# One list of rows per expert against two: first and second visits of a token in a fused attention and mixture-of-experts kernel

## The chip, the cores and the metric

The kernel runs on one core of one Trainium2 chip. The metric is the device time of one execution in microseconds (us). Each engine of the core has its own instruction stream: TensorE (PE) multiplies matrices, VectorE (DVE) and ScalarE (ACT) work elementwise, GpSimd (POOL) here issues the indirect transfers and the weight loads, and SyncE (SP) issues plain transfers. They wait for each other through semaphores.

## The reference, cut to what matters

Linear attention over q, k, v gives x with 4608 rows (tokens) of 512. A noisy router then chooses two of eight experts for each row, and the output is the weighted sum of the two experts' results.

```python
def _attn_ref(q, k, v):                  # each (8, 8, 576, 64)
    phi = lambda x: np.where(x > 0, x, np.exp(x) - 1.0) + 1.0
    q_p, k_p = phi(q), phi(k)
    kv = np.einsum('bhsd,bhse->bhde', k_p, v)
    z = np.sum(k_p, axis=2)
    num = np.einsum('bhsd,bhde->bhse', q_p, kv)
    den = np.einsum('bhsd,bhd->bhs', q_p, z)[..., None] + 1e-06
    return num / den
# x: (4608, 512); w1: (8, 512, 1024); w2: (8, 1024, 512)
logits = x @ w_gate
noisy_logits = logits + np.log1p(np.exp(x @ w_noise)) * noise
top2 = np.argpartition(-noisy_logits, 2, axis=1)[:, :2]
# top2_w: softmax over the two chosen logits
out = np.zeros((4608, 512))
for e in range(8):
    for k in range(2):
        mask = top2[:, k] == e
        h = np.maximum(x[mask] @ w1[e], 0.0)
        out[mask] += top2_w[mask, k, None] * (h @ w2[e])
```

The experts are computed in order of their number, so of a token's two experts the lower one is its first visit and the higher one its second.

## The kernel before

Attention and routing are done in groups of 1152 tokens. After each group, `dispatch` scatters its rows, with the gates and the token's number behind the 512 values, to `x_sorted`, a scratch array in device memory with one list for each expert:

```python
    def dispatch(self, u, a=0, z=9):

        tc = self.tc
        g, c0, c1 = UNITS[u]
        for ci in range(c0 + a, min(c1, c0 + z)):
            for sl in range(2):
                self.nc.gpsimd.nop()
                r = self.nc.gpsimd.indirect_dma_start(
                    out=self.x_sorted,
                    out_offset=bass.IndirectOffsetOnAxis(ap=self.r["posi", u][:, ci - c0, sl : sl + 1], axis=0),
                    in_=self.xr[g % 2][:, ci, :].bitcast(INT32), in_offset=None,
                )
# ...
```

Room for 1216 rows of each list is computed; a branch at the end handles longer lists. Experts 0 to 7 follow. A row tile of 128 passes four steps: load and transpose, `mm1` with w1 and relu, `mm2` with w2, and the output. Outside expert 0, each tile first clears a buffer `L`, then gathers what its tokens' first visit has written to `out` (a first visit's index lies out of bounds, so its row stays zero), adds, and scatters the sum to `out`:

```python
    def zero_l(self, b):
        for t in range(b["nt"]):
            b["L"][t] = self.lp.tile([P, HD], FP32, name="L")
            self.nc.vector.memset(b["L"][t][:], 0.0)

    def gather(self, b):

        nc, tc = self.nc, self.tc
        gi = self.m[b["key"]][2]
        for t in range(b["nt"]):
            m, tt = self.rows(b, t), b["t0"] + t
            nc.gpsimd.nop()
            r = nc.gpsimd.indirect_dma_start(
                out=b["L"][t][0:m].bitcast(INT32), out_offset=None, in_=self.out.bitcast(INT32),
                in_offset=bass.IndirectOffsetOnAxis(ap=gi[0:m, tt : tt + 1], axis=0),
                bounds_check=N_TOK - 1, oob_is_err=False,
            )
            g = f"own{b['e']}"
            tc.declare_no_dep(r.ins, group=g, reason="the rows of one expert are of distinct tokens")
            tc.add_to_no_dep_group(g, r.ins)

    def mm1(self, b, *fcs):
        nc, n = self.nc, b["n"]
        w1 = self.w[b["e"]][0]
        if "hT" not in b:
            b["hT"] = self.hp.tile([P, 8, 512], BF16, name="hT")
        for fc in fcs:
            ps = self.rot(self.ps_h, "h").tile([P, 512], FP32, name="b")
            for dc in range(4):
                nc.tensor.matmul(out=ps[:, 0:n], lhsT=w1[:, dc, fc * P : fc * P + P], rhs=b["xt"][:, dc, 0:n],
                                 start=(dc == 0), stop=(dc == 3))
            nc.scalar.activation(out=b["hT"][:, fc, 0:n], in_=ps[:, 0:n], func=ACT.Relu)

    def mm2(self, b, t):
        nc = self.nc
        w2 = self.w[b["e"]][1]
        m = self.rows(b, t)
        gate, tt = self.m[b["key"]][0], b["t0"] + t
        ps = self.rot(self.ps_y, "y").tile([P, HD], FP32, name="b")
        for fc in range(8):
            nc.tensor.matmul(out=ps[0:m], lhsT=b["hT"][:, fc, t * P : t * P + m], rhs=w2[:, fc, :],
                             start=(fc == 0), stop=(fc == 7))
        y = b["y", t] = self.rot(self.yp, "yy").tile([P, HD], FP32, name="y")
        if t in b["L"]:
            nc.vector.scalar_tensor_tensor(out=y[0:m], in0=ps[0:m], scalar=gate[0:m, tt : tt + 1],
                                           in1=b["L"][t][0:m], op0=ALU.mult, op1=ALU.add)
        else:
            nc.vector.tensor_scalar(out=y[0:m], in0=ps[0:m], scalar1=gate[0:m, tt : tt + 1], scalar2=None, op0=ALU.mult)

    def scatter(self, b, t):
        nc, tc = self.nc, self.tc
        m, tt = self.rows(b, t), b["t0"] + t
        si = self.m[b["key"]][1]
        nc.gpsimd.nop()
        r = nc.gpsimd.indirect_dma_start(
            out=self.out, out_offset=bass.IndirectOffsetOnAxis(ap=si[0:m, tt : tt + 1], axis=0),
            in_=b["y", t][0:m], in_offset=None, bounds_check=N_TOK - 1, oob_is_err=False,
        # ... (all scatters of an expert must have landed before the next expert gathers)
```

`interval` interleaves `mm1` of the current block (up to 512 rows) with `mm2` and the output of the block before. Two early blocks of expert 0, `r1` with 512 rows and `r2` with 256, are read before the dispatch is complete: after groups 1 and 2 the list's counter is raised to 512 and 768, so that later rows go behind that bound. Their rows are transposed by the DMA engines (`xt_load`); other blocks are transposed by TensorE (`xn_t`). At the end of the attention:

```python
    pa.ps_misc = pa.ps_misc[:1]
    col = c["rowpos"]
    pa.num(3, 0, 1)
    pa.num(3, 1, 0)
    pa.num(3, 1, 1)
    pa.num(3, 2, 0)
    pa.rt_a(3)
    pa.num(3, 2, 1)
    pa.rt_b(3)
    pb.mm1(r1, 0)
    pa.rt_c(3)
    pa.dispatch(3)
    pa.rt_a(4)
    pb.mm1(r1, 1)
    pa.rt_b(4)
    pb.mm1(r1, 2)
    pa.rt_c(4)
    pa.dispatch(4)
    pb.mm1(r1, 3, 4, 5, 6, 7)
    pb.meta("r1", c["cnt"][0][:], col[:, 0:4], code_of(0))
    pb.interval(r2, r1)
    pb.meta("r2", c["cnt"][1][:], col[:, 4:6], code_of(0))
    return r2
```

Then the blocks of the experts:

```python
        blocks = [pb.block(0, 768, CAP - 768, 0, 6, True)]
        for e in range(1, E):
            blocks += [pb.block(e, r, n, e, r // P) for r, n in ((0, 512), (512, 512), (1024, CAP - 1024))]
        pb.meta_load(0, 0, T_CAP)
        pb.xt_load(blocks[0])
        for i, b in enumerate(blocks):
            nxt = blocks[i + 1] if i + 1 < len(blocks) else None
            for nb in blocks[i + 1 : i + 3] if i == 0 else blocks[i + 2 : i + 3]:
                pb.xn_load(nb)
                if nb["row"] == nb["e"] * REGION:
                    pb.meta_load(nb["e"], nb["row"], T_CAP)
            if i == 0 or b["e"] != blocks[i - 1]["e"]:
                e = b["e"]
                pb.meta(e, c["carry"][:, e : e + 1], c["rowpos"][:], code_of(e))
            todo = []
            if e + 2 < E and (i == 0 or b["e"] != blocks[i - 1]["e"]):
                pb.w_tiles(e + 2, 1 if e + 2 < 6 else 0)
                todo = [(e + 2, part) for part in range(4)]
            pb.interval(b, prev, todo, nxt)
            prev = b
        pb.interval(None, prev)
    pb.overflow()
```

Of the kernel before, what the change touches and what calls it, by code (L numbers as in the profile page):

```python
# [7 lines left out]
FP32 = mybir.dt.float32  # L8
# [7 lines left out]
P = 128  # L16
# [6 lines left out]
CAP = 1216  # L23
T_CAP = 10

UNITS = [(0, 0, 9), (1, 0, 9), (2, 0, 9), (3, 0, 6), (3, 6, 9)]

ROUNDS = [(1, 512), (2, 768)]
REGION = N_TOK
ROW_W = 576  # L30
BIG = 1.0e6
# [8 lines left out]


def code_of(e):
    return float(E - e) / E


def build_constants(tc, consts, w_gate, w_noise, noise):
# [22 lines left out]
    )  # L69
    ut = c["ut"] = tile_("ut", [P, P], BF16)  # L70
# [25 lines left out]
    carry = c["carry"] = tile_("carry", [P, E])  # L96
    nc.vector.memset(carry[:], 0.0)
    c["cnt"] = [tile_(f"cnt{i}", [P, 1]) for i in range(len(ROUNDS))]
# [7 lines left out]
class PhaseA:  # L106


    def __init__(self, ctx, tc, q, k, v, x_sorted, psum):
        self.tc, self.nc = tc, tc.nc  # L110
        self.src, self.x_sorted = {"q": q, "k": k, "v": v}, x_sorted
        self.ps_num, self.ps_misc = psum
        self.turn = 0
        pool = lambda name, bufs: ctx.enter_context(tc.tile_pool(name=name, bufs=bufs, side="right"))
        self.kq = pool("A_kq", 3)
        self.pers = pool("A_pers", 1)
        self.v = [self.pers.tile([P, 12, S], BF16, name=f"v{i}") for i in range(2)]
        self.ep = pool("A_e", 2)
        self.kvp, self.kvt = pool("A_kvp", 2), pool("A_kvt", 1)
        self.pq = pool("A_pq", 5)  # L120
        self.rt = pool("A_rt", 1)
        self.x, self.e, self.kvps, self.kvbd, self.pqt, self.r, self.ps = {}, {}, {}, {}, {}, {}, {}
# [161 lines left out]
    def rt_b(self, u):  # L284
# [3 lines left out]
        t4 = lambda name, dt=FP32: self.rt.tile([P, 2, 9, E], dt, name=name)[:, :, 0:n]  # L288
# [3 lines left out]
        noisy, eq, oh, mx, code = t3("noisy"), t3("eq"), t4("oh"), t2("mx"), t2("code")  # L292
# [4 lines left out]
        for sl in range(2):  # L297
# [4 lines left out]
            nc.vector.tensor_tensor(out=oh[:, sl], in0=c8b, in1=bc(code, sl), op=ALU.is_equal)  # L302
            if sl == 0:
                nc.vector.scalar_tensor_tensor(out=noisy, in0=oh[:, 0], scalar=-1e30, in1=noisy,
                                               op0=ALU.mult, op1=ALU.add)
        A = t3("A", BF16)
        nc.vector.tensor_tensor(out=A, in0=oh[:, 0], in1=oh[:, 1], op=ALU.add)
        rps = self.misc()
        rk = rps[:, 0 : 8 * n].rearrange("p (a b) -> p a b", a=n)
        tt = rps[:, 256 : 256 + 8 * n].rearrange("p (a b) -> p a b", a=n)  # L310
        nc.tensor.matmul(out=rk, lhsT=c["ut"][:], rhs=A, start=True, stop=False, skip_group_check=True)
        nc.tensor.matmul(out=tt, lhsT=c["ones"][:], rhs=A, start=False, stop=False, skip_group_check=True)
# [3 lines left out]
        dl = t1("dlt")  # L316
        nc.vector.tensor_tensor(out=dl, in0=mx[:, 1], in1=mx[:, 0], op=ALU.subtract)
        meta = _ap(self.xr[g % 2], [[ROW_W, n], [1, 16]], off=c0 * ROW_W + HD).bitcast(FP32)
# [4 lines left out]
        nc.scalar.copy(out=fld(3), in_=code[:, 0])  # L323
        r.update(oh=oh, code=code, rps=rps, rk=rk, dl=dl)

    def rt_c(self, u):
# [3 lines left out]
        t2 = lambda name: self.rt.tile([P, 2, 9], FP32, name=name)[:, :, 0:n]  # L330
        pos, pr = self.rt.tile([P, 9, E], FP32, name="pos")[:, 0:n], self.rt.tile([P, 2, 9, E], FP32, name="pr")[:, :, 0:n]
        rank, posf, key = t2("rank"), t2("posf"), t2("key")
        tot, gs = self.rt.tile([P, E], FP32, name="tot"), self.rt.tile([P, 9], FP32, name="gs")[:, 0:n]
        nc.vector.tensor_scalar_add(out=gs, in0=r["dl"], scalar1=1.0 + 1e-9)
        nc.vector.reciprocal(out=gs, in_=gs)
        fld = r["fld"]
        nc.vector.tensor_tensor(out=pos, in0=r["rk"], in1=_ap(c["carry"], [[0, n], [1, E]]), op=ALU.add)
        nc.vector.tensor_tensor(out=fld(1), in0=r["dl"], in1=gs, op=ALU.mult)
        nc.vector.tensor_tensor(out=pr, in0=r["oh"], in1=_ap(pos, [[0, 2], [E, n], [1, E]]), op=ALU.mult)
        nc.vector.tensor_tensor(out=fld(2), in0=gs, in1=fld(1), op=ALU.subtract)  # L340
        nc.vector.tensor_reduce(out=rank, in_=pr, op=ALU.add, axis=AX.X)

        nc.vector.scalar_tensor_tensor(out=key, in0=rank, scalar=float(CAP), in1=r["code"],
                                       op0=ALU.is_ge, op1=ALU.subtract)
        nc.vector.scalar_tensor_tensor(out=posf, in0=r["code"], scalar=float(-REGION * E), in1=rank,
                                       op0=ALU.mult, op1=ALU.add)
        nc.vector.tensor_tensor(out=fld(4), in0=key[:, 0], in1=key[:, 1], op=ALU.is_lt)
        posi = r["posi", u] = self.rt.tile([P, 9, 2], INT32, name="posi", bufs=2)
        nc.vector.tensor_scalar_add(out=_ap(posi, [[1, 2], [2, n]]), in0=posf, scalar1=float(E * REGION))
        nc.vector.tensor_reduce(out=tot[:], in_=_ap(r["rps"], [[1, E], [E, n]], off=256), op=ALU.add, axis=AX.X)  # L350
        nc.vector.tensor_tensor(out=c["carry"][:], in0=c["carry"][:], in1=tot[:], op=ALU.add)
        for i, (after, q) in enumerate(ROUNDS):
            if after == u:
                c0_ = c["carry"][:, 0:1]
                nc.vector.tensor_copy(out=c["cnt"][i][:], in_=c0_)
                nc.vector.tensor_scalar_max(out=c0_, in0=c0_, scalar1=float(q))

    def dispatch(self, u, a=0, z=9):
# [3 lines left out]
        for ci in range(c0 + a, min(c1, c0 + z)):  # L362
            for sl in range(2):
# [7 lines left out]
                for i, (after, q) in enumerate(ROUNDS):  # L371
                    if after < u:
                        tc.declare_no_dep(r.ins, group=f"read{i}", reason="that round reads rows below its bound")
                tc.add_to_no_dep_group("disp", r.ins)


class PhaseB:


    def __init__(self, ctx, tc, w1, w2, x_sorted, out):  # L380
        self.tc, self.nc = tc, tc.nc
        self.w1, self.w2, self.x_sorted, self.out = w1, w2, x_sorted, out
# [5 lines left out]
        self.ps_h = self.ps_y = None  # L388
        self.count = {}
        self.w, self.m = {}, {}  # L390
# [22 lines left out]
    def meta_load(self, key, row, nt, group=None):  # L413
        m = self.mp.tile([P, nt, 8], INT32, name=f"meta{nt}")
        rows = self.x_sorted[row : row + nt * P, HD // 2 : HD // 2 + 8]
        r = self.nc.sync.dma_start(out=m[:], in_=rows.rearrange("(t p) c -> p t c", p=P))
        if group:
            self.tc.add_to_no_dep_group(group, r.ins)
        self.m[key] = (m, nt)

    def meta(self, key, n_e, rowpos, code):

        nc, mp = self.nc, self.mp
        mi, nt = self.m[key]
        m = mi[:].bitcast(FP32)
        t2 = lambda name, dt=FP32: mp.tile([P, nt], dt, name=f"{name}{nt}")
        gate, inv, isf, si, gi = t2("gate"), t2("inv"), t2("isf"), t2("si", INT32), t2("gi", INT32)
        nc.vector.tensor_scalar(out=inv[:], in0=rowpos, scalar1=n_e, scalar2=BIG, op0=ALU.is_ge, op1=ALU.mult)
        nc.vector.scalar_tensor_tensor(out=gate[:], in0=m[:, :, 3], scalar=code, in1=m[:, :, 2],
                                       op0=ALU.is_equal, op1=ALU.mult)  # L430
        nc.vector.scalar_tensor_tensor(out=isf[:], in0=m[:, :, 3], scalar=code, in1=m[:, :, 4],
                                       op0=ALU.is_equal, op1=ALU.is_equal)
        nc.vector.tensor_tensor(out=si[:], in0=mi[:, :, 0], in1=inv[:], op=ALU.max)
        nc.vector.tensor_tensor(out=gate[:], in0=gate[:], in1=m[:, :, 1], op=ALU.add)
        nc.vector.scalar_tensor_tensor(out=gi[:], in0=isf[:], scalar=BIG, in1=si[:], op0=ALU.mult, op1=ALU.max)
        self.m[key] = (gate, si, gi)

    def block(self, e, row, n, key, t0, first=False):
        return {"e": e, "row": e * REGION + row, "n": n, "key": key, "t0": t0, "first": first,
                "nt": -(-n // P), "L": {}}  # L440

    def xt_load(self, b, group=None):
        n = b["n"]
        b["xt"] = self.xp.tile([P, 4, 512], BF16, name="xt")
        src = self.x_sorted[b["row"] : b["row"] + n, 0 : HD // 2].bitcast(BF16)
        r = self.nc.sync.dma_start(out=b["xt"][:, :, 0:n], in_=src, transpose=True)
        if group:
            self.tc.add_to_no_dep_group(group, r.ins)

    def xn_load(self, b):  # L450

        n, nc = b["n"], self.nc
        b["xn"] = self.np.tile([P, 4, HD], BF16, name="xn")
        k = n // P
        src = lambda a, z: self.x_sorted[b["row"] + a : b["row"] + z, 0 : HD // 2].bitcast(BF16)
        nc.sync.dma_start(out=b["xn"][:, 0:k], in_=src(0, k * P).rearrange("(t p) d -> p t d", p=P))
# [361 lines left out]
```

## Time and profile before

| | us |
|---|---|
| median of 3 runs | 472.89 (471.3 to 472.99) |
| span of the profiled execution | 493.9 |
| TensorE busy | 367.1 (74%) |
| GpSimd busy | 269.7 (55%) |
| VectorE busy | 209.7 (42%) |
| ScalarE busy | 187.0 (38%) |
| scatters to x_sorted, 72 | 76.1 |
| scatters to out, 80 | 79.0 |
| gathers from out, 70 | 71.2 |
| clearing of L, 70 | 34.0 |

Times of single stretches are those of the profiled execution, which is longer than the timed runs. A row of the profile names the line of the kernel, the engine, the operation and the tiles (output <- input), how often it occurs, busy time and mean duration, and what ended the idle time before it. The chain of waits goes back from the last instruction of the execution, at each step to what released it. "issue" there is time in which an engine waited for nothing that the profile shows, and "another core or an unknown queue" a release that it can't name. PEclk is the clock granted to TensorE, where 1.00 is full speed. In the table by stage, the columns after the stretch and its length are busy us (and instructions) of PE, of its weight loads, of DVE, ACT and POOL, then the clock, the DMA share and GB/s.

### The profile page before, as it was taken

What the parts mean: (1) busy time and instruction counts of PE and PEld (TensorE: products, weight loads), DVE (VectorE), ACT (ScalarE), POOL (GpSimd) and SP (SyncE); (2) the same over time, 40 slices, a digit from 0 to 9 for tenths busy, and PEclk for the clock granted to TensorE, in tenths of its full rate; (3) what the DMA queues carried; (4) which work ended last, traced back from release to release, by engine and by line L of the source; (5) the groups of instructions that cost most, each with busy time, mean ns of one, the idle gap of its engine ahead of it and who ended that gap; (6) DMA issues with size and microseconds to landing.
All of it is one profiled execution on the core that took longest, in us unless ns stands there. A gap on an engine that the chain in (4) does not pass through costs nothing.

```text
span 493.9 us, 6809 instructions
## 1 busy us (share of the span) xinstructions
PE 367.1 (74%) x2513; PEld 208.2 (42%) x2513; DVE 209.7 (42%) x526; ACT 187.0 (38%) x304; POOL 269.7 (55%) x289
## 2 busy tenths in 40 slices
PE   0395354554332159999979999999997999999980
PEld 0284253443311014544634554554543554454540
DVE  1928999695672102431351351351260342242330
ACT  1537564513110022544325345345335336235310
POOL 6121258877667712437568547557467555546550
PEclk9997777666557559999998999999998999999995
DMA  9999993993974345395958846956956955434440
GB/s 138 207 238 210 208 224 96 216 211 109 167 214 141 119 84 162 114 225 116 212 175 165 205 149 144 240 152 145 249 183 152 255 182 156 144 126 116 156 142 2
DMA packets 69035, 82.12 MB, mean 166 GB/s; under 512 B 24981, under 2 KB 54997, under 8 KB 68992
## 3 DMA queue, kind: packets, MB, share of 16 engines
q0 software_dynamic: 40448, 69.90, 60.2%
q1 hardware_dynamic: 26880, 11.51, 10.6%
q10 hardware_dynamic: 1664, 0.18, 0.5%
q8 instruction: 21, 0.34, 0.3%
q14 instruction: 22, 0.18, 0.1%
HBM read 88.55 MB, written 31.74 MB: 244 GB/s over the span
## 4 chain that ended last, share of the span: by engine, by line
PE 62%; DVE 13%; DMA 10%; issue 4%; another core or an unknown queue 4%; ACT 4%; POOL 1%; POOLq 0%; ACTq 0%
PE b L512 29%; PE b L523 28%; DMA kq<-in_q_dram 7%; PE t L472 3%; DVE xr L254 3%; DMA x_sorted<-xr,posi 2%; DVE e L161 2%; ACT e L151 2%; PE num L243 1%; DVE kq L158 1%; DVE lwt L261 1%; DVE kvbd L192 1%; ACT hT L514 1%; PE misc L227 1%
## 5 line engine op out<-in xcount | busy, mean ns | idle before, releaser
L512 PE MATMUL b<-xt,w 128*128 128x512 bf16 (+3 forms) x768 | 158.1, 350 | 25.6 <-issue 19.3
L514 ACT ACTIVATE hT<-b 128x512 bf16<-128x512 f32 (+3 forms) x192 | 96.0, 510 | 163.2 <-PE b L512 110.4
L523 PE MATMUL b<-w,hT 128*128 128x512 bf16 (+1 forms) x640 | 150.9, 379 | 0.0
L537 POOL DMA_INDIRECT out_dram<-y,si x80 | 79.0, 988 | 99.0 <-DVE y L527 37.5
L527 DVE SCALAR_TENSOR_TENSOR y<-b,gate,L 128x512 f32<-128x512 f32 x70 | 51.5, 743 | 172.9 <-PE b L523 106.5
L512 PEld LDWEIGHTS <-w 128*128 128x128 bf16 x768 | 72.5, 101 | 94.8 <-issue 42.5
L365 POOL DMA_INDIRECT x_sorted<-xr,posi x72 | 76.1, 1057 | 34.2 <-issue 19.2
L495 POOL DMA_INDIRECT L<-out_dram,gi x70 | 71.2, 1017 | 38.1 <-issue 21.7
L523 PEld LDWEIGHTS <-hT 128*128 128x128 bf16 (+1 forms) x640 | 62.3, 99 | 69.0 <-issue 3.4
L151 ACT ACTIVATE e<-kq 128x2304 bf16<-128x2304 bf16 x16 | 33.1, 2122 | 21.2 <-DMA kq<-in_k_dram 9.2
L476 ACT COPY xt<-t 128x1024 bf16<-128x1024 bf16 x28 | 28.3, 1011 | 24.9 <-PE t L472 14.9
L486 DVE MEMSET L<- 128x512 f32 x70 | 34.0, 485 | 4.2 <-ACT xt L476 0.3
L180 PE MATMUL misc<-v,e 64*128 64x192 bf16 x144 | 19.9, 314 | 20.9 <-DVE e L161 20.9
L180 PEld LDWEIGHTS <-e 64*128 64x128 bf16 x288 | 21.6, 124 | 30.3 <-DVE e L161 28.7
L243 PE MATMUL num<-kvbd,pqt 128*64 128x162 bf16 x288 | 19.6, 311 | 19.5 <-DVE lwt L261 16.2
L472 PE MATMUL t<-ident,xn 128*128 128x128 bf16 x280 | 21.7, 219 | 6.0 <-ACT xt L476 6.0
L243 PEld LDWEIGHTS <-pqt 128*64 128x64 bf16 x288 | 16.2, 153 | 22.1 <-DVE lwt L261 13.1
L180 PE MATMUL b<-v,e 64*128 64x192 bf16 x144 | 20.0, 314 | 7.0 <-DVE e L161 4.9
L472 PEld LDWEIGHTS <-xn 128*128 128x128 bf16 x280 | 18.5, 99 | 15.3 <-issue 6.6
L254 DVE TENSOR_TENSOR xr<-num,rden 128x384 bf16<-128x384 f32 x48 | 23.4, 550 | 0.4
L161 DVE TENSOR_TENSOR e<-e,kq 128x2304 bf16<-128x2304 bf16 x16 | 21.3, 1354 | 0.3
L530 DVE TENSOR_SCALAR y<-b,gate 128x512 f32<-128x512 f32 (+1 forms) x10 | 7.5, 750 | 27.2 <-PE b L523 27.2
(108 smaller groups left out, 214.5 us busy)
## 6 DMA issues: line engine op xcount, KB each, us to landing
w<-in_moe_w_dram POOLq DMA_DIRECT2D x32, 512.0 KB
xn<-x_sorted SPq DMA_DIRECT2D x14, 512.0 KB
kq<-in_k_dram POOLq DMA_DIRECT2D x8, 576.0 KB
kq<-in_q_dram POOLq DMA_DIRECT2D x8, 576.0 KB
v<-in_v_dram POOLq DMA_DIRECT2D x8, 576.0 KB
out_dram<-y,si POOLq DMA_INDIRECT x80
x_sorted<-zrow SPq DMA_DIRECT2D x8, 144.0 KB
x_sorted<-xr,posi POOLq DMA_INDIRECT x72
```

Of the source, the lines that this page charges most:

```text
L151: self.nc.scalar.activation(out=e, in_=x, func=ACT.Exp)
L180: nc.tensor.matmul(out=self.kvps[g, h, j][:, KVM * i : KVM * i + KVM], lhsT=e[half, hp, ci, :], rhs=v[half, hp::4, 64 * ci : 64 * ci + 64] ...
L243: nc.tensor.matmul(out=ps[half, hp, KVW * i : KVW * i + KVW], lhsT=self.pqt[g, 3 * t + i][:, hp, half], rhs=self.kvbd[g][:, j, hp, :], sta ...
L254: nc.vector.tensor_tensor(out=_ap(xr, [[ROW_W, 3], [256, 2], [1, 64]], off=3 * t * ROW_W + 64 * hp), in0=_ap(ps, [[KVW, 3], [64, 2], [1, 6 ...
L365: r = self.nc.gpsimd.indirect_dma_start(out=self.x_sorted, out_offset=bass.IndirectOffsetOnAxis(ap=self.r["posi", u][:, ci - c0, sl : sl + ...
L472: nc.tensor.transpose(ps[:, i, dc, 0:m], b["xn"][0:m, t, dc * P : dc * P + P], self.c["ident"][0:m, 0:m])
L495: r = nc.gpsimd.indirect_dma_start(out=b["L"][t][0:m].bitcast(INT32), out_offset=None, in_=self.out.bitcast(INT32), in_offset=bass.Indirec ...
L512: nc.tensor.matmul(out=ps[:, 0:n], lhsT=w1[:, dc, fc * P : fc * P + P], rhs=b["xt"][:, dc, 0:n], start=(dc == 0), stop=(dc == 3))
L514: nc.scalar.activation(out=b["hT"][:, fc, 0:n], in_=ps[:, 0:n], func=ACT.Relu)
L523: nc.tensor.matmul(out=ps[0:m], lhsT=b["hT"][:, fc, t * P : t * P + m], rhs=w2[:, fc, :], start=(fc == 0), stop=(fc == 7))
L527: nc.vector.scalar_tensor_tensor(out=y[0:m], in0=ps[0:m], scalar=gate[0:m, tt : tt + 1], in1=b["L"][t][0:m], op0=ALU.mult, op1=ALU.add)
L537: r = nc.gpsimd.indirect_dma_start(out=self.out, out_offset=bass.IndirectOffsetOnAxis(ap=si[0:m, tt : tt + 1], axis=0), in_=b["y", t][0:m] ...
```

## The change

Each expert gets two lists: F, the rows for which it is the first visit, and S, those for which it is the second. A first visit no longer touches `out`: its result is stored plainly to a scratch array `part`, in the order of the list. A second visit gathers the token's row of `part`, adds, and writes `out` once. Nothing has to be cleared, and no gather waits for scatters to `out`. A row carries where its first visit lies. Expert e computes `N_F[e]` full tiles of F, `N_S[e]` of S, and 192 "mid" rows (M), gathered from the ends of both lists; expert 0 has only F and expert 7 only S. Three experts, not one, have early rows in two rounds: 512, 384 and 256 rows of experts 0, 1 and 2, then up to 768, 640 and 512. A memset of a spare tile on GpSimd now follows each indirect transfer. The weights of experts 0 and 1 are loaded between dispatches of groups 1 and 2. No row is transposed by DMA engines any more.

The core of the diff (cut; the router's ranking now counts 16 lists in the same way):

```diff
-ROUNDS = [(1, 512), (2, 768)]
+N_F = [8, 7, 6, 5, 3, 2, 1, 0]
+N_S = [8 - n for n in N_F]
+ROUNDS = [(1, (512, 384, 256)), (2, (768, 640, 512))]
+EARLY = 3
 # constants
+    c["gap"], c["gap2"] = tile_("gap", [P, 192]), tile_("gap2", [P, 352])
 # dispatch, after each scatter
+    def apart(self):
+        self.nc.gpsimd.memset(self.c["gap"][:], 0.0)
 # attention, in the loop over groups
-        pa.dispatch(g, 0, 6 if g == 0 else 9)
-        if g > 0:
-            rd = (r1, r2)[g - 1]
-            pb.meta_load(rd["key"], (0, 512)[g - 1], rd["nt"], f"read{g - 1}")
-            pb.xt_load(rd, f"read{g - 1}")
+        if g == 0:
+            pa.dispatch(0, 0, 6)
+        else:
+            pb.w_tiles(g - 1)
+            for i in range(4):
+                pa.dispatch(g, 2 * i, 2 * i + 2)
+                pb.w_load(g - 1, i)
+            pa.dispatch(g, 8, 9)
 # gather, for S and M tiles alone
-            r = nc.gpsimd.indirect_dma_start(
-                out=b["L"][t][0:m].bitcast(INT32), out_offset=None, in_=self.out.bitcast(INT32), ...
+            if kind == "F":
+                continue
+            L = b["L"][t] = self.lp.tile([P, HD], FP32, name="L")
+            nc.gpsimd.nop()
+            r = nc.gpsimd.indirect_dma_start(
+                out=L[0:m].bitcast(INT32), out_offset=None, in_=self.part.bitcast(INT32), ...
+            nc.gpsimd.memset(self.c["gap2"][:], 0.0)
 # the output of a tile
-    def scatter(self, b, t):
+    def put(self, b, t):
+        if kind != "S":
+            row = e * REGION + (N_F[e] if kind == "M" else 0) * P + i * P
+            r = nc.sync.dma_start(out=self.part[row : row + m], in_=y[0:m])
+        if kind != "F":
+            nc.gpsimd.nop()
+            r = nc.gpsimd.indirect_dma_start(out=self.out, ...)     # as before
+            nc.gpsimd.memset(self.c["gap2"][:], 0.0)
 # interval
-        if cur and new and not cur["first"]:
-            self.gather(cur)
+        if nxt:
+            self.gather(nxt)
 # the end of the routing, with the early blocks
+    a0, a1 = first, pb.block(1, ("F", 0, 3))
+    b0, b1 = pb.block(0, ("F", 4, 2)), pb.block(1, ("F", 3, 2))
+    a2, c0 = pb.block(2, ("F", 0, 4)), pb.block(0, ("F", 6, 4))
+    ...
+    pb.mm1(a0, 0)
+    pa.rt_b(3)
+    pb.mm1(a0, 1, 2)
+    pa.rt_c(3)
+    pa.dispatch(3)
+    pa.rt_a(4)
+    pb.mm1(a0, 3, 4, 5)
+    pa.rt_b(4)
+    pb.mm1(a0, 6, 7)
+    pa.rt_c(4)
+    pa.dispatch(4)
+    pb.mids()
+    ...
+    pb.interval(a1, a0, (), b0)
+    pb.w_load(2, 0, 1, 2, 3)
+    pb.interval(b0, a1, (), b1)
+    pb.prepare(0)
+    pb.xn_load(c0)
+    pb.interval(b1, b0, (), a2)
+    pb.w_tiles(3, 1)
+    pb.w_load(3, 0, 1, 2, 3)
+    pb.interval(a2, b1, (), c0)
 # the later blocks: kind, first tile, tiles
+PLAN = {
+    1: [[("F", 5, 2)], [("M", 0, 1), ("S", 0, 1), ("M", 1, 1)]],
+    2: [[("F", 4, 2)], [("M", 0, 1), ("S", 0, 2), ("M", 1, 1)]],
+    3: [[("F", 0, 4)], [("F", 4, 1), ("M", 0, 1), ("S", 0, 1), ("M", 1, 1)], [("S", 1, 2)]],
+    ...
+    7: [[("S", 0, 4)], [("S", 4, 4)], [("S", 8, 2)]],
+}
```

## What was predicted

> **What bounds the kernel now.** I read the 40 slices first, then busy time by stage, the chain of work in order of time, the waits, and the GpSimd timeline. The slices show two kernels in one.
>
> ```profile
> PE   0395354554332159999979999999997999999980
> POOL 6121258877667712437568547557467555546550
> PEclk9997777666557559999998999999998999999995
> ```
>
> From slice 15 (185 us) on, TensorE is nearly always busy at full clock: the experts are bound by it. Before, during attention and routing, it is mostly idle at a reduced clock, while GpSimd is busiest in slices 7 to 13, where it scatters rows to the sorted lists. The stage table (length, then busy us of each engine) sets the sizes:
>
> ```profile
> 137.00:155.00 18.00, 7.31 (x27) 2.64 (x27) 11.54 (x58) 2.53 (x10) 12.12 (x13) 0.61 0.58 183
> 155.00:181.00 26.00, 4.03 (x9) 1.22 (x9) 2.87 (x22) 2.14 (x4) 15.80 (x17) 0.56 0.34 107
> 181.00:480.00 299.00, 289.39 (x1664) 148.24 (x1662) 97.67 (x204) 122.88 (x229) 167.62 (x173) 0.98 0.67 169
> 480.00:494.00 14.00, 0.00 (x0) 0.00 (x0) 0.17 (x1) 0.00 (x0) 0.92 (x1) 0.58 0.06 22
> ```
>
> From 155 to 181 us TensorE works 4 us of 26. The chain says how:
>
> ```profile
> 151.04 3.77 PE b L512 x8
> 154.81 9.11 issue
> 163.92 0.60 ACT hT L514
> 164.52 9.88 another core or an unknown queue
> 174.42 0.60 ACT hT L514
> 175.02 5.02 another core or an unknown queue
> 180.06 0.61 ACT hT L514
> 180.70 4.42 PE b L512 x12
> ```
>
> The first block of expert 0 has begun, but ScalarE and VectorE hardly advance, with no wait the profile can name. The stretch lies over GpSimd's unbroken row of dispatch scatters and ends with them:
>
> ```profile
> 173.46 0.96 POOL L365 DMA_INDIRECT x_sorted<-xr,posi  x1 [0.30 <-issue]
> 174.72 0.96 POOL L365 DMA_INDIRECT x_sorted<-xr,posi  x1 [0.30 <-issue]
> 188.55 0.99 POOL L537 DMA_INDIRECT out_dram<-y,si  x1 [12.87 <-DVE y L530]
> ```
>
> A scatter takes 0.96 and 0.30 passes before the next, so 1.27 us each. Even without stalls, only 768 early rows of expert 0 could be computed before the last scatter lands. Later, the read-modify-write of the output costs something too. GpSimd's longest waits in the expert stage:
>
> ```profile
> POOL L L495 <- DMA out_dram<-y,si: 14.6, 5, 6.2
> POOL out_dram L537 <- issue: 10.1, 31, 0.9
> POOL out_dram L537 <- DVE gate L429: 6.9, 5, 2.3
> ```
>
> The first line is five gathers of a new expert held up by the scatters of the old one; VectorE additionally waits 14.8 us for gathers at L527. TensorE itself lists only about 12 us of waits after 181 us.
>
> [...] granted clock 0.50 from 175 to 185 us, and the twelve matmuls from 180.70 take 4.42 us, 0.37 each, against 0.216 later. [...] From 120 to 200 us each instruction queue shows one packet, so I don't take the stall for a shortage of instructions.
>
> **The change part by part.** (1) *TensorE work.* Eight experts keep 1216 rows and ten tiles each. Up-projection: 8 x 1216 x 32 columns, or 608 matmuls of 512 columns at 0.216 us (eight take 1.73 us in the chain): 131 us. Down-projection: 80 tiles x 1.73: 138 us. Transposes: three DMA transposes become forty more on TensorE, 320 in all, eight in 0.44 us: 18 us, of which 2.2 are new. Sum 287 us, nearly unchanged; smaller blocks (256, 320, 384 columns) cost nothing extra, since eight matmuls of 192 columns already take only 0.67 us.
>
> (2) *Early rows.* Instead of 512 + 256 rows of expert 0, 512 + 256 of expert 0, 384 + 256 of expert 1 and 512 of expert 2 may be computed before the dispatch has ended: 1920 rows. A row costs 64 columns, so 1920 x 64 x 0.422 ns = 52 us, plus 3 for transposes, against 21 before. Work for 34 us more is available exactly where TensorE stood idle.
>
> (3) *Dispatch.* A GpSimd memset of 192 elements now follows each of 72 scatters. A memset of 128 elements took 0.20 us and one of 1 element 0.10, so I estimate 0.25 us for 192, and 72 x 0.25 = 18 us. Weight loads of experts 0 and 1 move between scatters, adding nothing overall. The last scatter thus moves from 176 to about 188 us: attention leaves slack at first, and roughly 12 of the 18 us show. If the unbroken row of scatters is what holds up the others, the spaces also release ScalarE and VectorE.
>
> (4) *What early work waits for.* TensorE starts at about 144 us, as now. [...] The second early round needs the third group's scatters, about 160 us, and its load, about 166; TensorE reaches it at 159: 7 us lost. Expert 2's weights are issued only after the last scatter. Four loads of 1 MB each took some 15 us to land after 93 us, so the first two land near 198, while TensorE arrives near 190: 8 us lost.
>
> (5) *Expert stage.* The 70 memsets of L (34 us of VectorE) go, off the path. Indirect transfers fall from 150 to 104: 46 gathers, 46 scatters and 12 for mixed tiles; 46 plain stores go to SyncE. GpSimd needs 104 x (1.0 + 0.3 + about 0.38) = 175 us, against about 195 before, in a stage of some 270: not a bound. A gather now waits only for plain stores of earlier experts and is issued a block ahead. TensorE lost 299 - 289 = 10 us idle plus about 6 at low clock; I leave 6 in all.
>
> (6) *End.* Last scatter and final test stay: 14 us.
>
> Sum for a profiled execution: 144 + 287 + 3 + 7 + 8 + 6 + 14 = 469, against 493.9: 25 us less. The timed runs before are 21 us below the profiled span. Some of the unnamed stall may exist only under the profiler, so I do not carry all 25 over, but 19: 472.9 - 19 = 454 us.
>
> **The rivals.** *The stall belongs to the profiler.* The 21 us between profile and timed runs are suspiciously like the stall of 26. Then the timed kernel before already did all its 21 us of early work and waited only for the dispatch; the gain is the wait left over, some 15 us, minus the later dispatch: 465 to 472. Against it: the spaces in the new code suggest that closely packed transfers hurt something. *The dispatch becomes the bound.* If memset and switching cost 0.6 us and not 0.25, the last scatter lands near 205 us, the weights of expert 2 near 222, and TensorE stands idle again: 470 to 480. For it: GpSimd is the busiest engine from 65 to 176. *Stores and gathers collide.* SyncE takes stores and row loads in order, so a store waiting for VectorE delays the next load; TensorE would show short waits in every expert. Rows are loaded two blocks ahead, which speaks against it; three microseconds an expert would give 478. *Better than thought.* The attention stage also has stalls of 3.5 and 3.4 us near 117 to 125, in the chain, within a row of scatters; spaces may remove these, and the experts may lose nothing: 441.
>
> **Range and chances.** The central sum gives 454. The good rival and half of its gain again set the lower end, 439; the profiler rival sets the upper end, 470. Faster by over 2% means below 463.4: I give 0.70. Within 2%: 0.19. Slower needs dispatch or SyncE to become a bound: 0.11.
>
> **What would show it.** Right: TensorE busy most of 150 to 210 us; the last dispatch near 188; scatter spacing near 1.5 us; no unnamed waits of ScalarE for 10 us; expert stage 290 us or less from there on; GpSimd's waits for out_dram gone. Wrong: first matmul of expert 0 well after 144 (attention delayed by spaced dispatches), spacing of 1.8 or more, TensorE waiting for w over 15 us at expert 2, or repeated waits for xn, xm or L in later experts. If the stall is gone but the timed gain is under 10 us, the profiler rival was right.

## The result, and the profile after

The changed kernel takes 455.35 us (median of 4 runs, 454.04 to 456.05). Beside it the kernel before takes 472.22 us (471.3 to 472.99). The ratio is 0.964, with a 95% interval from 0.9609 to 0.9671. Ratios, here and below, leave out disturbed executions, so that those of `b_pet` and of the runs on chip 10 are not quite the quotients of the medians. The profiled span is 453.6 us. The number predicted was 454, and the range held it; the reasons need more sorting than that suggests.

The same three rows of the 40 slices as before (now 11.3 us each):

```profile
PE   0195475564626879799999999999999899999991
POOL 7130229888888888710065637469658867776883
PEclk9998868668558899899999999999999999999997
```

TensorE is busy from slice 12 (137 us) on and no longer from slice 15 (185 us). The hole with digits 3, 3, 2 and 1 is gone, although GpSimd's row of scatters (slices 6 to 15) is denser than it was. The table by stage:

```profile
137.00:145.00 8.00, 6.68 (x30) 3.00 (x31) 3.69 (x23) 4.32 (x11) 7.05 (x12) 0.78 0.86 216
145.00:181.00 36.00, 29.83 (x182) 17.24 (x185) 11.88 (x55) 13.24 (x28) 31.74 (x51) 0.95 0.72 213
181.00:211.00 30.00, 26.65 (x153) 13.60 (x155) 2.60 (x6) 14.15 (x25) 10.99 (x16) 0.94 1.12 223
211.00:440.00 229.00, 226.15 (x1343) 121.99 (x1365) 54.87 (x114) 100.54 (x190) 148.18 (x208) 1.00 0.72 191
440.00:454.00 14.00, 4.38 (x20) 1.77 (x18) 2.25 (x3) 0.00 (x0) 5.48 (x9) 0.78 0.22 80
```

From 137 to 181 us TensorE works 36.5 us of 44; before, it worked 11.3 in the same stretch. All that it waits for between 137 and 215 us, one row for each cause (total, times, longest):

```profile
PE t L586 <- DMA xn<-x_sorted: 2.8, 2, 2.3
PE misc L331 <- DVE A L326: 2.3, 1, 2.3
PE b L624 <- DMA w<-in_moe_w_dram: 2.1, 1, 2.1
PE b L624 <- ACT xt L590: 1.3, 2, 1.1
PE t L586 <- ACT xt L590: 1.3, 2, 1.1
PE b L624 <- ACT xt L592: 0.7, 1, 0.7
PE b L624 <- issue: 0.4, 2, 0.2
```

Between 60 and 215 us no unnamed wait ("issue", or "remote": another core or an unknown queue) above 0.2 us is left on TensorE, ScalarE and VectorE. Last, GpSimd's timeline at the end of the dispatch; the bracket is the idle time before the instruction:

```profile
177.74 0.97 POOL L387 DMA_INDIRECT x_sorted<-xr,posi  x1 [0.16 <-issue]
178.71 0.28 POOL L378 MEMSET gap<- 128x192 f32 x1
179.15 0.97 POOL L387 DMA_INDIRECT x_sorted<-xr,posi  x1 [0.17 <-issue]
```

One scatter starts 1.41 us after the other (1.27 before). The memset takes 0.27, but the idle time ahead of a scatter falls from 0.30 to 0.17, so the memset costs 0.14 us net. The last scatter starts at 179.15; in the profile of before it was 174.72.

### The profile page after: what moved, and what is told of

It reads as the page before. It is cut to its first block, busy times and chain, and to the rows that moved or that the text cites. A ratio compares the mean times of both kernels' runs of the same rounds, so it can differ in the third digit from the quotient of the medians.

```text
span 453.6 us, 7034 instructions
## 1 busy us (share of the span) xinstructions
PE 361.4 (80%) x2554; PEld 215.8 (48%) x2585; DVE 179.3 (40%) x481; ACT 193.0 (43%) x313; POOL 285.4 (63%) x425
## 4 chain that ended last, share of the span: by engine, by line
PE 38%; POOL 29%; DMA 18%; issue 5%; DVE 5%; ACT 2%; POOLq 0%; ACTq 0%; DVEq 0%
PE b L624 18%; PE b L635 18%; POOL x_sorted L387 14%; DMA kq<-in_q_dram 8%; POOL gap L378 4%; POOL L L607 4%; DMA w<-in_moe_w_dram 3%; DMA xn<-x_sorted 3%; POOL out_dram L655 3%; PE t L586 3%; DMA xm<-x_sorted,m_idx 2%; ACT e L169 2%; POOL gap L614 2%; POOL gap L661 1%; DMA x_sorted<-xr,posi 1%
## 5 line engine op out<-in xcount | busy, mean ns | idle before, releaser
L624 PE MATMUL b<-xt,w 128*128 128x512 bf16 (+5 forms) x787 | 148.7, 333 | 5.3 <-DMA w<-in_moe_w_dram 2.1
L626 ACT ACTIVATE hT<-b 128x512 bf16<-128x512 f32 (+5 forms) x200 | 97.0, 496 | 113.5 <-PE b L624 111.6
L590 ACT COPY xt<-t 128x1024 bf16<-128x1024 bf16 x32 | 32.4, 1012 | 56.3 <-PE t L586 56.0
L655 POOL DMA_INDIRECT out_dram<-y,si x34 | 33.9, 997 | 14.4 <-DVE y L639 8.9
L607 POOL DMA_INDIRECT L<-part,mgi x12 | 12.0, 1004 | 49.0 <-DMA xn<-x_sorted 35.6
L607 POOL DMA_INDIRECT L<-part,gi x34 | 34.7, 1021 | 9.2 <-issue 9.2
L586 PE MATMUL t<-ident,xn 128*128 128x128 bf16 (+1 forms) x256 | 20.9, 221 | 4.2 <-DMA xn<-x_sorted 2.8
L586 PEld LDWEIGHTS <-xn 128*128 128x128 bf16 (+1 forms) x256 | 17.3, 99 | 13.4 <-DMA xn<-x_sorted 3.8
L655 POOL DMA_INDIRECT out_dram<-y,msi x12 | 11.7, 979 | 18.9 <-DVE y L639 13.7
L639 DVE SCALAR_TENSOR_TENSOR y<-b,mgate,L 128x512 f32<-128x512 f32 (+1 forms) x12 | 9.0, 746 | 32.8 <-PE b L635 32.8
```

Of the source, the lines that this page charges most:

```text
L586: nc.tensor.transpose(ps[:, i, dc, 0:m], self.xn(b, t, dc), self.c["ident"][0:m, 0:m])
L590: nc.scalar.copy(out=b["xt"][:, :, t * P : t * P + 2 * P].rearrange("p c (i r) -> p i c r", i=2), in_=ps)
L607: r = nc.gpsimd.indirect_dma_start(out=L[0:m].bitcast(INT32), out_offset=None, in_=self.part.bitcast(INT32), in_offset=bass.IndirectOffset ...
L655: r = nc.gpsimd.indirect_dma_start(out=self.out, out_offset=bass.IndirectOffsetOnAxis(ap=self.m[e, kind, i]["si"][0:m], axis=0), in_=y[0:m ...
```

## The experiments

**Theory A:** the time before is set by the last dispatch scatter, behind which TensorE has nothing to do; early rows of three experts fill that wait, and the memsets cost what they delay. **Rival B:** the memsets (called spaces from here) end the unnamed stall, and that is the gain. **Rival C:** the gain lies in the output path, in gathers that no longer wait for scatters. **Rival D:** the gain is the transposes taken from the DMA engines.

The runs fell on four chips, and these differ. On chip 7 the kernel before takes 472.5 us, as in the result above; on chips 13, 10 and 15 it takes 492 to 494. So each ratio below is against the kernel before on the same chip.

### Chip 7: spaces added, spaces removed, early rows removed

`b_gap`: the kernel before, with one line more.

```diff
                     in_=self.xr[g % 2][:, ci, :].bitcast(INT32), in_offset=None,
                 )
+                self.nc.gpsimd.memset(self.c["gap"][:], 0.0)     # 128 x 192, a spare tile
```

> The kernel before, with the memset of 192 elements after each of the 72 dispatch scatters and nothing else. Theory A (the unnamed stall from 155 to 181 us exists only under the profiler; the timed kernel before waits for the last scatter): the profiled span falls by 15 to 25 us from 493.9, because the stall goes, while the timed median does not fall; it rises by 3 to 10 us, since 72 x 0.135 us (1.405 against 1.27 us a scatter) put the last scatter about 10 us later. Theory B (the spaces release ScalarE and VectorE in timed runs too): the timed median falls by 8 us or more. Theory C (two lists make the gain): the timed median stays within 3 us.

Measured: 481.5 us against 472.54, ratio 1.0196 (1.0167 to 1.0226). The last scatter starts at 183.99 us. The spacing is 1.405 us instead of 1.27, so 72 spaces make 72 x 0.135 = 9.7 us of later dispatch, and the time grows by 9.0. That fits a kernel that its dispatch bounds almost one to one (9.7 is worked out; the kernel before was not profiled on chip 7). Rival B is wrong for this chip; spaces alone cost. Two stages of this run, and what TensorE and then GpSimd waited for:

```profile
145.00:193.00 48.00, 24.08 (x98) 10.76 (x99) 9.72 (x55) 8.67 (x21) 39.52 (x62) 0.71 0.47 147
193.00:465.00 272.00, 270.22 (x1560) 140.15 (x1591) 92.46 (x187) 118.08 (x218) 162.38 (x169) 0.99 0.70 179
```

```profile
PE b L514 <- DMA xt<-x_sorted: 29.4, 3, 13.3
```

```profile
POOL L L497 <- DMA out_dram<-y,si: 31.8, 8, 8.4
```

This decides on rival C too. In the experts GpSimd waits 31.8 us for scatters to `out` before it may gather, and TensorE still works 270.2 of 272 us: these waits lie beside the matmuls. In this stretch the old output path cost TensorE at most 1.8 us. TensorE's long waits from 137 us on, 29.4 us together, are for transposed rows: before the first early matmul (12.6), in the second round (3.5), and behind the last early row:

```profile
193.03 3.17 PE L514 MATMUL b<-xt,w 128*128 128x448 bf16 x8 [13.33 <-DMA xt<-x_sorted]
```

This last wait is mostly one for the dispatch: the rows are loaded from 187.01 us on, after the last scatter.

`a_nogap1` and `a_nogap`: the changed kernel without the 72 spaces of the dispatch, and without these and the memsets behind the later gathers and scatters.

```diff
     def apart(self):
-        self.nc.gpsimd.memset(self.c["gap"][:], 0.0)
+        pass
 # a_nogap alone, three places:
-            nc.gpsimd.memset(self.c["gap2"][:], 0.0)
```

> The changed kernel without the memset after the dispatch scatters; the memsets after the later gathers and scatters stay. Theory A: timed 450 to 457 us, as with it or slightly faster, since the last scatter comes some 10 us earlier and TensorE hardly waits for it; the profiled span grows by 10 us or more above 453.6, because the stall returns. Theory B: the timed median rises by 8 us or more, to 463 or above.

> The changed kernel without any of the memsets, neither after dispatch scatters nor after the later gathers and scatters. Theory A: 448 to 457 us timed, no worse than the changed kernel. Theory B: 463 us or more, and more than without the first kind alone if closely packed gathers and scatters hold up the experts as well.

Measured: 447.86 us, ratio 0.9471 (0.9413 to 0.9528), and 445.82, ratio 0.9436 (0.9412 to 0.9461). The profile of `a_nogap` has no unnamed wait of ScalarE or VectorE between 60 and 215 us, though its scatters stand 1.27 us apart. On this chip the spaces cost 7 to 10 us of the 455. The last scatter starts at 169.73 in `a_nogap`, 9.4 us earlier, but that is not how they cost: the changed kernel has early rows until 208 us, and TensorE doesn't wait for the last scatter. It starts its early work 4.2 us later with spaces (133.5 and 137.76), and then idles 10.8 us up to 211 instead of 7.2 up to 199. The memsets in the expert stage are not told apart from nothing: the intervals of the two runs overlap.

`a_early1`: the changed kernel, spaces kept, with early rows of expert 0 alone.

```diff
-ROUNDS = [(1, (512, 384, 256)), (2, (768, 640, 512))]
-EARLY = 3
+ROUNDS = [(1, (512,)), (2, (768,))]
+EARLY = 1
-    pb.interval(a1, a0, (), b0)
-    pb.interval(b1, b0, (), a2)
-    pb.interval(a2, b1, (), c0)
+    pb.interval(b0, a0, (), c0)      # rows of experts 1 and 2 move to the later blocks
```

> The changed kernel with early rows of expert 0 alone (512, then up to 768); the early blocks of experts 1 and 2 are computed after the dispatch, in order of experts. Two lists, plain stores and all memsets stay. Theory A (early rows make the gain): TensorE has 21 us of work instead of 52 while the scatters run, so 467 to 480 us, most or all of the gain gone. Theory C (two lists and plain stores make the gain by freeing gathers from scatters): 455 to 461 us.

Measured: 491.78 us, ratio 1.0424 (1.0391 to 1.0457), 36 us more than the changed kernel. TensorE's waits from 130 us on:

```profile
PE t L587 <- DMA xn<-x_sorted: 26.2, 2, 22.9
PE t L587 <- DMA x_sorted<-xr,posi: 13.8, 1, 13.8
```

It confirms the direction of theory A; its 36 us overstate the size. Early work starts at 137.08, as in the changed kernel, but from 148.2 on TensorE waits 13.8 us for rows of the second round. After 171.35 it waits another 22.9 for the first late rows:

```profile
194.22 1.04 PE L587 MATMUL t<-ident,xn 128*128 128x128 bf16 x8 [22.87 <-DMA xn<-x_sorted]
```

Only part of that second wait comes from the missing early rows. The load of these rows (181.80) goes out among loads of 8 MB of weights (from 179.94 on), and behind the wait, in TensorE's order, stand 16 matmuls of `mm1` and two tiles of `mm2`, some 5.2 us of early work that `b_gap` does ahead of its wait. In `a_early1_ng` below, where these weights come later, TensorE has such rows 7.2 us after the last scatter starts; with that, the wait would end at 186.0, 8.2 us sooner. So I estimate 491.8 - 8.2 - 5.2, about 478 us, without these two flaws of my edit. That is near the 481.5 of `b_gap`: without the early rows of experts 1 and 2, two lists, plain loads and TensorE transposes together bring a few us at most, and with them the kernel takes 455. This speaks against rivals C and D as causes of their own on chip 7.

### Chip 13: the stall is there

`b_again`: the kernel before, unchanged. `b_pet`: the kernel before, whose three DMA transposes are replaced by a plain load and transposes on TensorE.

```diff
-            pb.xt_load(rd, f"read{g - 1}")          # DMA transpose
+            pb.xn_load(rd, f"read{g - 1}")          # plain load
+    pb.xn_t(r1, 0)                                  # 128 x 128 transposes on TensorE
+    pb.xn_t(r1, 1)
+    pb.xn_t(r2, 0)
```

> The kernel before, unchanged, profiled once more. If the unnamed stall of ScalarE and VectorE is a habit of this kernel under the profiler, the profiled span is again 485 to 500 us with unnamed waits between 150 and 185 us. If it was an accident of that one profile, the span is 468 to 476 us and TensorE's waits in that stretch are named, for the transposed rows.

> The kernel before with its three DMA transposes replaced: the rows of the early blocks and of the first late block are loaded plainly and transposed by TensorE, as in the changed kernel. Everything else stays. With 192-element memsets added, TensorE waited 12.6 and 13.3 us for the first and the third transposed load. Theory A (the last dispatch scatter is the bound): 466 to 473 us, since only the wait after the last scatter shortens, by up to 6 us. Theory D (the DMA transposes make a large part of the gain): 464 us or less. If the DMA transposes beside packed scatters make the unnamed stall, the profiled span is within 3 us of the timed median.

Measured: `b_again` 494.54 us in one execution, beside 493.37 (492.34 to 494.66, 7 runs) for the same kernel. `b_pet` 490.6 (484.55 to 500.81), ratio 0.9864 (0.9805 to 0.9923); its profiled execution was the longest of the four. The chain of `b_again` shows the pieces known from the profile of before, at nearly the same places:

```profile
151.30 3.00 PE b L512 x4
154.31 8.47 issue
162.78 0.60 ACT hT L514
163.37 9.90 issue
173.28 0.60 ACT hT L514
173.87 5.72 another core or an unknown queue
179.61 0.60 ACT hT L514
```

And these pieces now stand in timed runs of 493 us. So what I had taken for a cost of profiling belongs to the place where the kernel ran: the first profile of before, with its span of 493.9 (that execution took 495.78 us), was most likely taken on such a chip, while its timed runs of 472 were not. `b_pet` keeps the stall (ScalarE waits 7.2 us for "issue" and 14.4 for "remote" ahead of two copies of the transposed rows), so the stall occurs without DMA transposes too. Rival D explains no more than the 1.4% here.

`a_early1_ng` and `a_early2_ng`: the changed kernel without any memsets, with early rows of one expert and of two; in the first the weights of experts 2 and 3 come later.

```diff
 # against the changed kernel, both
-                self.apart()
 # a_early1_ng
-EARLY = 3
+EARLY = 1
 # a_early2_ng
-EARLY = 3
+EARLY = 2
```

> The changed kernel with early rows of expert 0 alone, no memsets, and the weights of experts 2 and 3 loaded only after the first late rows, so that two lists and TensorE transposes remain as the only differences from the kernel before. Last scatter near 171 us, rows of the next block near 178, then some 292 us. Theory A: 466 to 475 us, the same as the kernel before within 1.5%. Theory C (two lists make the gain): 462 us or less.

> The changed kernel without memsets and with early rows of experts 0 and 1 alone (1408 rows, 38 us of TensorE from about 134 us, to about 182 with warm-up and waits). Without memsets the first late rows should be there near 178. Theory A (early work only has to reach the last scatter's rows): 444 to 451 us, as with three experts. If each early row gains by itself, it lies halfway to one expert's 466 to 475, near 458.

Measured: 484.7 us, ratio 0.9819 (0.9795 to 0.9842), and 478.17, ratio 0.9701 (0.9668 to 0.9735). Both show the stall (VectorE waits 16.0 us for "remote" in the first, ScalarE 14.2 in the second), and both lie above all that was expected, so they are no clean measure of the early rows. Their difference of 6.5 us speaks for a second expert with early rows, though the order of the weight loads differs too. A gain from the third is not shown: with all three and no memsets, `a_nogap_2` below has a ratio of 0.9729 (0.9642 to 0.9816), no lower than the 0.9701 with two.

### Chip 10: what the spaces are for

The question was now whether the spaces, which cost 7 to 10 us on chip 7, pay on a chip with the stall. `after2` is the changed kernel, `a_nogap_2` that without any memsets, `b_gap_2` the kernel before with spaces; the edits are those shown above.

> The changed kernel unchanged, on the chip of the two runs beside it. The question is what the memsets between the scatters do on a chip on which the unnamed stall occurs in timed runs (there the kernel before took 493 us). Theory 'spaces prevent the stall': on such a chip the changed kernel takes what it took elsewhere, 454 to 460 us, a ratio of 0.92 to 0.935, and its profile has no unnamed wait of ScalarE or VectorE of 5 us or more. Rival 'spaces do nothing for the stall': the stall shows in this profile too, and the time is 468 to 480. On a chip where the kernel before takes about 472, this repeats the known 455 and tells nothing of the question.

> The changed kernel without any of the memsets, once more, beside the changed kernel on the same chip. Where the kernel before takes about 493 us: theory 'spaces prevent the stall' expects 462 to 475 with unnamed waits of 10 us or more in the row of scatters, slower than the changed kernel; the rival expects it 5 to 10 us faster than the changed kernel, as on the chip where it took 445.8. Where the kernel before takes about 472: 446 under both.

> The kernel before with a memset of 192 elements after each dispatch scatter, and nothing else, once more. Where the kernel before takes about 493 us: theory 'spaces prevent the stall' expects 480 to 485, as on the other chip, thus faster than the kernel before by 8 to 13 us; the rival expects 500 or more (9 us of later dispatch on top of the stall). Where the kernel before takes about 472: 481 under both.

Measured, with the kernel before at 492.3 us there (485.43 to 499.68, 23 runs): `after2` 462.03, ratio 0.9339 (0.9261 to 0.9417); `a_nogap_2` 480.85, ratio 0.9729 (0.9642 to 0.9816); `b_gap_2` 489.93, ratio 1.0005 (0.9966 to 1.0044). Removing the memsets, which gained 7 to 10 us on chip 7, loses 19 here. The chain of `a_nogap_2` shows where:

```profile
159.70 3.64 another core or an unknown queue
163.37 0.60 ACT hT L624
163.97 6.43 another core or an unknown queue
170.42 0.60 ACT hT L624
171.02 9.28 another core or an unknown queue
180.32 1.02 ACT xt L589
```

Three gaps of ScalarE, 19.4 us together, end at about the time when the dispatch does (its last scatter starts at 176.1). From 145 to 182 us TensorE works 12.9 us of 37, against 30.5 of the 37 from 133 to 170 in the same kernel on chip 7. In `after2` TensorE works 31.2 us of the 41 from 145 to 186. ScalarE has one unnamed wait above 1 us there; others are 6.3 and 5.7 us of VectorE and 2.8 of TensorE:

```profile
176.11 0.49 ACT L626 ACTIVATE hT<-b 128x384 bf16<-128x384 f32 x1 [3.82 <-remote]
```

So the spaces shorten the stall and don't remove it, and neither expectation for `after2` was met: the changed kernel is 6.7 us above its 455.35 here, that without memsets 35.0 above its 445.82. In `b_gap_2` the stall is only partly gone (ScalarE still waits 17.0 us for "remote" ahead of `pqt`, a tile of the attention, and 13.4 ahead of `hT`), and what the spaces save and what they delay about cancel. I had expected 480 to 485 there, and missed.

### Chip 15: half of the spaces

```diff
-                self.apart()
+                if sl == 1:
+                    self.apart()
```

> The changed kernel with a memset after every second dispatch scatter only, 36 of 72, all else as changed. It should end its dispatch about 36 x 0.135 = 5 us sooner than the changed kernel. Where the kernel before takes about 472 us (no stall): 450 to 452, halfway between the changed kernel at 455.4 and the one without dispatch memsets at 446 to 448. Where it takes about 492 (stall): if what matters is that the row is broken now and then, there is as little stall as with all memsets, 456 to 461, ratio 0.926 to 0.937; if every pair of packed scatters adds its share, half of the 19 us between no memsets (480.9) and all (462.0) comes back, 468 to 474, ratio 0.95 to 0.962.

Measured: 466.33 us (463.6 to 468.19), ratio 0.9422 (0.9333 to 0.951), the kernel before at 494.38. It lies between the two expectations, and its interval overlaps both them and that of `after2`; two gaps of ScalarE are left, 11.4 us ahead of `pqt` and 8.0 ahead of `hT`. In these two profiles half the spaces leave longer gaps than all of them, but the run doesn't settle whether they cost more time, nor how the stall grows.

All together, medians in us, with the chip in brackets:

| spaces in the dispatch | kernel before | changed kernel |
|---|---|---|
| none, no stall | 472.5 (7) | 445.8 (7, no memsets at all) |
| 72, no stall | 481.5 (7) | 455.4 (beside 472.2) |
| none, stall | 493.4 (13), 492.3 (10), 494.4 (15) | 480.9 (10, no memsets at all) |
| 36, stall | | 466.3 (15) |
| 72, stall | 489.9 (10) | 462.0 (10) |

On chip 7 the kernel without memsets beats both given ones; on chip 10, with the stall, the changed kernel does. No version measured is best on both.

**What stays open** is what the stall is. It isn't VectorE's alone: in the chain of `a_nogap_2` ScalarE stands for up to 9.28 us at a time, and in `b_again` one of TensorE's unnamed waits lasts 8.7. One more observation: with the stall, the trace itself has holes. It holds 3,492 completion records of transfers for `a_nogap_2` and 5,456 for `a_nogap`, for the same 63 thousand packets; between 160 and 180 us 31 against 305. All runs on chips 13, 10 and 15 hold 3,247 to 4,067; those on chip 7 and the changed kernel's first run 5,392 to 5,473. The profile of before holds 3,391, which fits a chip with the stall. That records are missing is measured; that an engine stands for the same reason is only a guess of mine, and no run shows it. And where records are lost, an "issue" or "remote" may hide a releaser whose record is missing: that the engines stand is certain, not that they wait for nothing known. Each timed execution has its span and granted clock on record as well, so none of these runs tells whether an unrecorded one would stall.

## Why the prediction was right, step by step

The number was right; of its two parts one was too high and one too low. The sum for the profiled execution was 469 and the profile says 453.6, 15 us less. Then I took the timed run to be 15 us shorter than that, because before it was 21 us shorter; in fact it is as long as the profile (455.35). The two errors cancelled, which was luck.

(1) *TensorE work, 287 us:* holds. From 137 to 454 us it is busy 293.7 us, with the last of the attention and the slower clock (0.78 to 0.95 up to 211 us) in it.

(2) *Early rows, 34 us more work for the idle stretch:* holds where there is no stall, and the gain there needs them. From 137 us to about the first block without an early row, I compare `b_gap` (which has the same spaces and no stall on TensorE's path; its stretch from 145 to 193 us stands above) with the changed kernel:

```profile
137.00:145.00 8.00, 0.00 (x0) 0.00 (x0) 1.15 (x7) 0.00 (x0) 4.08 (x8) 0.50 1.31 182
```

```profile
137.00:211.00 74.00, 63.16 (x364) 33.83 (x371) 18.17 (x83) 31.72 (x63) 49.78 (x77) 0.93 0.90 217
```

That is 56 - 24.1 = 31.9 us in `b_gap` and 74 - 63.2 = 10.8 in the changed kernel: 21 of the 26 us between their spans (479.8 and 453.6). Another 4.9 lie behind the last matmul (14.1 and 9.2 us); why, no run shows. The 21 are not the early rows' alone: the first matmul on early rows starts at 148.28 in `b_gap` and at 137.76 in the changed kernel, 10.5 us sooner. In `a_early1` the same early start only made TensorE wait later, so it gains where enough early rows follow. The changed kernel with its old DMA transposes was not run, so the two shares stay open. Without spaces on both sides, the change gains 472.5 - 445.8 = 26.7 us on chip 7 (`a_nogap`); the spaces give 9.5 of them back.

In part this was luck. In the profile of before, TensorE still had early rows of expert 0 to do at 180.70 us, when ScalarE went on after its gaps. More early rows alone could not have filled that stretch. Only where nothing stalls do they run out ahead of the dispatch (the last wait of 13.33 us in `b_gap`). The prediction says so in one sentence ("Even without stalls"), but it took the size of the hole from the profile with the stall.

(3) *Dispatch, 72 x 0.25 = 18 us:* the term mis-sized. The memset was 0.27 us, near enough, but I added it to an unchanged idle time of 0.30. That fell to 0.17, so a scatter grew by 0.135 and all by 9.7 us, and the last started at 179 instead of 188. I also let only 12 us show; `b_gap` shows 9.0 of 9.7.

(4) *Start of the early work at 144, and 18 us of waits and warming up:* too pessimistic everywhere. I had booked the transposes as 2.2 us more for TensorE, and not that the rows might come earlier. In `b_gap` the first DMA transpose is issued at 130.00 and keeps SyncE's queue 14.24 us; the first matmul starts at 148.28. In the changed kernel the plain load is issued at 129.28, TensorE transposes at 133.51 and the first matmul starts at 137.76.

```profile
130.00 14.24 SPq L448 DMA_TRANSPOSE xt<-x_sorted  x1
161.95 1.66 SPq L448 DMA_TRANSPOSE xt<-x_sorted  x1
187.01 2.52 SPq L448 DMA_TRANSPOSE xt<-x_sorted  x1
```

```profile
133.51 1.03 PE L586 MATMUL t<-ident,xt 128*128 128x128 bf16 x8 [6.24 <-DMA xt<-x_sorted]
137.76 0.59 PE L624 MATMUL b<-xt,w 128*128 128x512 bf16 x1 [1.10 <-ACT xt L590]
```

So 18.3 us pass from issue to first matmul in the one and 8.5 in the other. It isn't the transpose alone that is slow: in `b_gap` the later ones, of 256 and 448 rows, take 3.8 and 6.0 us to the first matmul. The first of 512 rows ran beside four weight loads issued from 128.12 us on, which the changed kernel spreads out; and for the plain load of the same rows TensorE waited 9.85 us in `a_nogap1`, 6.24 in the changed kernel. What held it up is not shown. The second early round waited 2.3 us instead of 7, the weights of expert 2 2.1 instead of 8. The sum also held 3 us for a lower clock at the start, which was my estimate; measured is a granted clock of 0.67 from 137.76 to 142 us and of 0.96 from 142 to 181.

(5) *Expert stage, 6 us lost:* 229 - 226.2 = 2.9. Gathers wait 7.7 us for plain stores and 35.6 for row loads, beside the path. (The three waits of GpSimd that the prediction calls the longest were not: 37.5 and 25.0 us went to VectorE's results; nothing in its sum rests on it.) The remark that the old read-modify-write "costs something too" is refuted by the 270.2 of 272 us in `b_gap`: the two lists make early rows of several experts possible, and in this stretch bring TensorE 1.8 us at most beside that.

(6) *End, 14 us:* the last matmuls end at 444.4, so 9.2.

*The rivals.* "The stall belongs to the profiler" was the rival that I should have followed further: its arithmetic (the timed kernel before did its 21 us of early work and waited only for the dispatch) describes chip 7, where the stall was absent; on three other chips the stall was in the timed runs. It gave 465 to 472, because it counted the 18 us of later dispatch and left out that the new early rows fill the wait. "The dispatch becomes the bound" and "stores and gathers collide" did not happen. SyncE's queue did take stores and row loads in order (in the changed kernel a store waits 11.1 us for VectorE until 271.13, and the row load behind it is issued at 272.91), but from 211 to 440 us TensorE waits 1.3 us for gathered rows and for no others. "Better than thought" counted on the spaces to remove stalls; where 455 was measured there was none to remove, and they lengthen the time.

## What to carry to other kernels

If a stage of one engine (here GpSimd's 72 scatters) holds up all others, give these work that needs only a part of its result, and compare the idle time of the bound engine before and after; a wait that looks large on another engine (31.8 us ahead of gathers in `b_gap`) cost TensorE 1.8 us at most. Before explaining a gap between a profile and timed runs, run the same kernel again elsewhere: the kernel before took 472.5 us on one chip and 492 to 494 on three, and in one stretch of 37 us TensorE worked 30.5 us in `a_nogap` and 12.9 in the same kernel as `a_nogap_2`. A remedy like the spaces must be measured in both surroundings, because here it cost 7 to 10 us in one and saved 19 in the other.

## What the runs showed of the hardware

- On chips 13 and 10, an unbroken row of indirect transfers 1.27 us apart goes with engines standing still with no wait that the profile can name, ScalarE for up to 14.4 us at a time (`b_pet`), VectorE for 16.0 (`a_early1_ng`) and TensorE for 8.7 (`b_again`), in traces that have lost records; the kernel before takes 492 to 494 us there and on chip 15, 472.5 on chip 7. At 1.41 us apart the changed kernel loses 6.7 us on chip 10, at 1.27 us 35.
- A memset of 0.27 us between two indirect transfers moves the next by only 0.135, because the idle time between instructions shrinks from 0.30 to 0.17.
- From the issue of a DMA transpose to the first matmul on its rows 18.3 us passed for 512 rows of 512 bf16 values, beside four weight loads, and 3.8 and 6.0 us for 256 and 448 rows later (`b_gap`). A plain load of the 512 rows and transposes on TensorE took 8.5 us in the changed kernel, where TensorE waited 6.24 us for the load; in `a_nogap1` it waited 9.85.
